# First gates of a gated recurrence one step earlier, x through GpSimd's queue, and an evenly paced weight conversion

## The chip, the cores and the metric

One core of one Trainium2 chip. The metric is the device time of one execution in microseconds (us); lower is better. Before: 490.97 us median of 3 runs (490.67 to 492.67). The engines are called as the profile calls them: PE is TensorE, DVE VectorE, ACT ScalarE, POOL GpSimd, SP SyncE.

## The reference

```python
# attention: batch 4, 8 heads, 768 positions, head size 48
for t in range(S):
    state = alpha[:, :, t, :, None] * state + einsum('bhd,bhe->bhde', k[:, :, t], v[:, :, t])
    y[:, :, t] = einsum('bhd,bhde->bhe', q[:, :, t], state)
# its output, as x (3072 tokens x 384), through a multiplicative feed-forward block
a = x @ w1          # 384 x 1024
b = x @ w2          # 384 x 1024
h = a * b @ w3      # 1024 x 1024
return h @ w_out    # 1024 x 384
# the weights are float64 in the inputs
```

## The kernel before

The sequence is cut into 24 chunks of 128 positions. **Part 1** works through them, one step n each. A step has a chain of its own: logarithm of the decay (L246, ACT), its running sum (L261, PE), exponentials (L267 and L268, ACT), their product with k and q (qk, L277, DVE), transposition (L299, PE, and its copy L301, ACT), scores (L339, PE), mask (ms, L342, DVE), attention (L364, PE), copy of the result (L368, ACT). The result, x, goes to DRAM (L236, in the next step) and comes back transposed for the **gates** (L379), in groups of three chunks. A gate half is an exact product out of three parts: six matmuls (L396), a copy (L398, ACT), three matmuls (L400), a combination (L401, DVE). Before a group's first gate its x is split in three (L385 ACT, L386 and L387 DVE).

```python
def load_x(g, queue=nc.sync):
    st["xT", g] = xp.tile([C, KM, TG], FP32, tag="xT", name="xT")
    queue.dma_start(out=st["xT", g], in_=xd[g].rearrange("(k p) t -> p k t", p=C))

def split_x(g, i):
    x = st.pop(("xT", g))
    t = tr[i].tile([C, 3, KM, TG], FP32R, tag="x3", name="x3")
    st["x3", g] = t
    nc.scalar.activation(t[:, 0], x, AF.Copy, scale=1.0 - 2.0 ** -13)            # L385
    nc.vector.tensor_sub(t[:, 1], x, t[:, 0].bitcast(FP32))                       # L386
    nc.vector.scalar_tensor_tensor(t[:, 2], t[:, 0].bitcast(FP32), 1.0 + 1.0 / P, x,
                                   op0=ALU.mult, op1=ALU.subtract)                # L387
```

Beside all that, the float64 weights are converted to fp32 by integer operations on ACT (L189, L194, L207) and DVE (3.68 us for a block), a bit in each call of `convert`. The loop that paces it:

```python
begin = {4 + 4 * g: (g, range(FH if g < 4 else KF)) for g in range(5)}

for n in range(N + 1):
    store()                       # x of the step before to DRAM, by SyncE
    ... loads of v, alpha, k and q ahead ...
    if n:
        attend_state(n - 1)
    if n < N:
        scores(n)
    transposed(n + 1)
    if n - 2 in begin:
        g, tiles = begin[n - 2]
        split_x(g, 0)
        fill.extend(gate(g, f) for f in tiles)
    pieces = (0, 3, 3, 2)[(n - 6) % 4] if n > 5 else 0
    if n == 0:
        logs(2); decays(2); logs(3)
    early = n < 7
    convert(1, 2 if n == 0 else 3)
    advance(n)
    if n:
        attend(n - 1)
    outer(n)
    run(pieces > 0)               # half a gate from the list `fill`
    if early:
        convert(1)
    decayed(n + 2)
    logs(n + 4)
    if n in begin:
        load_x(begin[n][0])
    convert(early and n > 2)
    run(pieces > 1)
    decays(n + 3)
    convert(early or n % 3 == 0)
    run(pieces > 2)
```

## Time and profile before

| | before |
|---|---|
| time, median of the first 3 runs | 490.97 us |
| span of the profiled run | 492.8 us |
| PE busy | 462.0 us, 94% |
| DVE busy | 371.0 us, 75% |
| first mask of step 11 | 94.2 us |
| first gates (L396) | 62.59 us |

The page's slices are fortieths of the span; a digit is the busy share in tenths. The rows of a stretch give its length, then busy time and number of instructions of PE, PEld, DVE, ACT and POOL, then the granted clock of TensorE (1.00 is full speed, 0.50 would be half all the time), the DMA share and GB/s. A line of a timeline gives start and length, engine, line and operation, output and inputs; in brackets how long the engine stood idle before it and what ended that. The lines themselves are shown in the prediction.

One thing to know of this profile: its run took 494.63 us, some 3 us above its neighbours. It was one execution.

### The profile page before, as it was taken

To read this page: it belongs to the slowest core of one execution; us is meant where nothing else is said; L and a number is where in the kernel's file an instruction comes from. 1 tells how busy PE (TensorE), PEld (TensorE's weight loads), DVE (VectorE), ACT (ScalarE), POOL (GpSimd) and SP (SyncE) were. 2 spreads that over 40 slices of the span, in tenths; PEclk is the share of its full clock that TensorE was granted. 3 is DMA by queue.
4 is the path that set the end of the run, shared out by engine and by line. 5 is a ranking of instruction groups with operands and counts; after the bars stand their busy time and mean duration, and the time that the engine had idled before them with its cause. 6 is when DMAs were issued, how large, how long until landed. Compare 5 with 4: busy or idle time off the path is not lost.

```text
span 492.8 us, 9909 instructions
## 1 busy us (share of the span) xinstructions
PE 462.0 (94%) x3760; PEld 422.5 (86%) x3760; DVE 371.0 (75%) x620; ACT 250.1 (51%) x479; POOL 37.5 (8%) x83
## 2 busy tenths in 40 slices
PE   3788689999998979999999999999999999999997
PEld 1566479888998968999999988888888999999996
DVE  2779899887988684999999769686433786667771
ACT  2767677676765563555556444444222533333330
POOL 2132132021103100000000000000000000000000
PEclk9989999999999998999999999999999999999999
DMA  9999999899999963666454433320001875555511
GB/s 176 185 200 205 236 199 201 217 183 234 194 227 189 214 207 101 175 183 195 158 195 155 156 117 118 118 92 32 33 32 61 229 225 176 177 176 178 176 49 48
DMA packets 160495, 79.10 MB, mean 161 GB/s; under 512 B 104640, under 2 KB 154304, under 8 KB 160448
## 3 DMA queue, kind: packets, MB, share of 16 engines
q1 hardware_dynamic: 159168, 78.40, 62.7%
q0 software_dynamic: 1280, 0.08, 0.4%
q8 instruction: 29, 0.48, 0.4%
q14 instruction: 18, 0.15, 0.1%
HBM read 56.40 MB, written 22.06 MB: 159 GB/s over the span
## 4 chain that ended last, share of the span: by engine, by line
PE 73%; DVE 9%; DMA 8%; SPq 4%; issue 3%; ACT 2%; POOL 0%; DVEq 0%; POOLq 0%; ACTq 0%
PE bank L396 37%; PE bank L400 18%; PE bank L445 8%; DMA raw<-in_moe_w_dram 3%; PE bank L339 2%; PE bank L364 2%; DVE ms L342 2%; PE bank L439 1%; DMA xT<-xd 1%; DMA abd<-ab 1%; DMA dec<-ends 1%; PE bank L299 1%; SPq L130 1%; DVE qk L277 1%; SPq L124 1%
## 5 line engine op out<-in xcount | busy, mean ns | idle before, releaser
L396 PE MATMUL bank<-x,w 128*128 128x384 f32 x768 | 159.3, 341 | 0.0
L396 PEld LDWEIGHTS bank<-x,w 128*128 128x128 f32 x768 | 134.6, 188 | 3.5 <-issue 0.5
L398 ACT ACTIVATE t<-bank 128x384 f32<-128x384 f32 x152 | 74.5, 492 | 109.7 <-PE bank L396 97.8
L401 DVE SCALAR_TENSOR_TENSOR r<-bank,t 128x384 f32<-128x384 f32 x128 | 69.7, 555 | 34.0 <-ACT t L398 32.1
L400 PE MATMUL bank<-x,w 128*128 128x384 f32 x384 | 87.3, 335 | 0.4 <-DVE x L387 0.4
L396 PE MATMUL bank<-w3o,ab 128*128 128x384 f32 x384 | 70.4, 334 | 0.0
L400 PEld LDWEIGHTS bank<-x,w 128*128 128x128 f32 x384 | 68.3, 188 | 0.7 <-issue 0.7
L396 PEld LDWEIGHTS bank<-w3o,ab 128*128 128x128 f32 x384 | 66.9, 188 | 0.0
L445 PE MATMUL bank<-wo,w3T 128*128 128x384 f32 x128 | 42.6, 486 | 0.0
L189 ACT ACTIVATE rest<-raw 128x512 f32<-128x512 uint32 (+1 forms) x36 | 23.4, 651 | 33.0 <-DMA raw<-in_moe_w_dram 20.5
L412 DVE TENSOR_TENSOR ab<-r 128x384 f32<-128x384 f32 x64 | 35.6, 556 | 2.3 <-DMA abd<-ab 1.5
L400 PE MATMUL bank<-w3o,ab 128*128 128x384 f32 x192 | 37.1, 334 | 0.0
L445 PEld LDWEIGHTS bank<-wo,w3T 128*128 128x128 f32 x128 | 24.2, 189 | 14.9
L464 DVE TENSOR_TENSOR ab<-abl,ab 128x1024 fp32r<-128x1024 f32 x24 | 29.4, 1224 | 9.2 <-ACT ab L463 9.2
L339 PEld LDWEIGHTS bank<-qkT 48*128 48x128 f32 x384 | 25.4, 200 | 12.4 <-ACT qkT L301 5.7
L339 PE MATMUL bank<-qkT 48*128 48x128 f32 x384 | 30.3, 299 | 6.0 <-ACT qkT L301 4.3
L463 ACT ACTIVATE ab<-abl 128x1024 fp32r<-128x1024 f32 x24 | 25.5, 1064 | 19.0 <-PE bank L400 18.8
L400 PEld LDWEIGHTS bank<-w3o,ab 128*128 128x128 f32 x192 | 33.6, 188 | 0.0
L342 DVE TENSOR_TENSOR ms<-bank,keep 128x512 int32<-128x512 int32 x48 | 31.1, 684 | 1.7 <-PE bank L339 1.7
L194 ACT ACTIVATE power<-power,rebias 128x512 uint32<-128x512 uint32 (+1 forms) x36 | 25.3, 705 | 12.2 <-DVE power L193 12.2
L401 DVE SCALAR_TENSOR_TENSOR o<-bank,t 128x384 f32<-128x384 f32 x24 | 13.4, 557 | 22.4 <-issue 13.7
L277 DVE TENSOR_TENSOR qk<-kq,e 128x768 f32<-128x768 f32 x24 | 22.9, 953 | 9.5 <-ACT e L268 7.2
(69 smaller groups left out, 540.1 us busy)
## 6 DMA issues: line engine op xcount, KB each, us to landing
abd<-ab SPq DMA_DIRECT2D x64, 192.0 KB, 2.7
abl<-abd SPq DMA_DIRECT2D x24, 512.0 KB, 4.5
raw<-in_moe_w_dram SPq DMA_DIRECT2D x16, 512.0 KB, 3.9
xT<-xd SPq DMA_DIRECT2D x12, 576.0 KB, 4.2
raw<-in_moe_w_dram SPq DMA_DIRECT2D x24, 256.0 KB, 4.8
ac<-in_alpha_dram SPq DMA_DIRECT2D x24, 192.0 KB, 5.0
kq<-in_k_dram SPq DMA_DIRECT2D x24, 192.0 KB, 5.4
kq<-in_q_dram SPq DMA_DIRECT2D x24, 192.0 KB, 4.3
```

The lines of the kernel that those rows point to most:

```text
L194: nc.scalar.activation(power, power, AF.Relu, scale=2.0 ** 23, bias=rebias)
L277: nc.vector.tensor_mul(qks[n % 3][:, :, :, 0:D], st.pop(("kq", n)), st.pop(("e", n)).rearrange("p i (h d) -> p i h d", h=H))
L339: nc.tensor.matmul(sc[i][:, j, :], qkT[r, 0, j, :], qkT[r, 1, j, :], start=True, stop=True)
L342: nc.vector.tensor_tensor(ms[:, i].bitcast(I32), sc[i].bitcast(I32), keep_bc, op=ALU.bitwise_and)
L396: nc.tensor.matmul(p1, w[part][i], x[part][i], start=(part == i == 0), stop=(part == 1 and i == n - 1))
L398: nc.scalar.activation(t, p1, AF.Copy, scale=(1.0 + 1.0 / P) * scale)
L400: nc.tensor.matmul(p2, w[2][i], x[2][i], start=(i == 0), stop=(i == n - 1))
L401: nc.vector.scalar_tensor_tensor(to, p2, -scale, t, op0=ALU.mult, op1=ALU.add)
L412: nc.vector.tensor_mul(ab, *r)
L445: nc.tensor.matmul(po, w3T[:, j, :], wo[:, j, :], start=(j == 0), stop=(j == KF - 1))
L463: nc.scalar.activation(t[:, 0], ab, AF.Copy, scale=1.0 - 2.0 ** -13)
L464: nc.vector.tensor_sub(t[:, 1], ab, t[:, 0].bitcast(FP32))
```

## The change

The intent: the first group's gates fill TensorE's pauses from the seventh step on, two halves in each of four steps, in place of 0+3+3+2 from there; x of part 1's groups is loaded by GpSimd's queue, so that SyncE's other loads do not stand behind it; the conversion has an even pace; logarithms and qk come earlier in their step, and the split logarithm has a second buffer. The letters A to E below are: A the second buffer, B the first group's gates, C x by GpSimd, D the order of logs and qk, E the pace of `convert`. (They are not the rivals (A) to (D) of the prediction.)

```diff
--- before.py
+++ after.py
@@ -246,7 +246,7 @@
         nc.scalar.activation(la, a, AF.Ln)
         if n >= LATE:
 
-            t = st["la", n] = work.tile([C, 2, DM], FP32R, tag="la2", name="la2", bufs=1)
+            t = st["la", n] = work.tile([C, 2, DM], FP32R, tag="la2", name="la2")
             nc.scalar.copy(t[:, 0], la)
             nc.vector.tensor_sub(t[:, 1], la, t[:, 0].bitcast(FP32))
         if n in ends:
@@ -505,7 +505,14 @@
     load_a(4)
 
 
-    begin = {4 + 4 * g: (g, range(FH if g < 4 else KF)) for g in range(5)}
+    first = 4
+    begin = {first + 4 * g: (g, range(FH if g < 4 else KF)) for g in range(5)}
+
+    def visit(n):
+        g, tiles = begin[n]
+        split_x(g, 0)
+        fill.extend(gate(g, f) for f in tiles)
+
 
     for n in range(N + 1):
         store()
@@ -517,33 +524,33 @@
         if n < N:
             scores(n)
         transposed(n + 1)
-        if n - 2 in begin:
-            g, tiles = begin[n - 2]
-            split_x(g, 0)
-            fill.extend(gate(g, f) for f in tiles)
-        pieces = (0, 3, 3, 2)[(n - 6) % 4] if n > 5 else 0
+        if n - 2 in begin and n - 2 != first:
+            visit(n - 2)
+        pieces = 0 if n <= first + 1 else 2 if n < first + 6 else (0, 3, 3, 2)[(n - first - 2) % 4]
         if n == 0:
             logs(2)
             decays(2)
-            logs(3)
-        early = n < 7
+
+        if n < 4:
+            logs(n + 3)
+        if n > 2:
+            logs(n + 4)
+        decayed(n + 2)
         convert(1, 2 if n == 0 else 3)
         advance(n)
+        if n in begin:
+            load_x(begin[n][0], nc.gpsimd)
         if n:
             attend(n - 1)
         outer(n)
         run(pieces > 0)
-        if early:
-            convert(1)
-        decayed(n + 2)
-        logs(n + 4)
-        if n in begin:
-            load_x(begin[n][0])
-        convert(early and n > 2)
+        convert(n > 0)
         run(pieces > 1)
         decays(n + 3)
-        convert(early or n % 3 == 0)
+        convert(n < 9)
         run(pieces > 2)
+        if n - 1 == first:
+            visit(first)
     store()
     part1.close()
```

## The prediction

> **What bounds the kernel now.** I read the page first (busy shares and slices), then the busy time per stretch, then the timelines of TensorE, VectorE and ScalarE over the first 200 us.
>
> The page, engine shares and slices of 12.3 us:
>
> ```profile
> PE 462.0 (94%) x3760; PEld 422.5 (86%) x3760; DVE 371.0 (75%) x620; ACT 250.1 (51%) x479; POOL 37.5 (8%) x83
> ...
> PE   3788689999998979999999999999999999999997
> ...
> DVE  2779899887988684999999769686433786667771
> ...
> PEclk9989999999999998999999999999999999999999
> ```
>
> TensorE (PE) is the bound of the whole: idle 492.8 - 462.0 = 30.8 us. The change removes no matmul, so a gain can only come out of these 30.8 us and out of matmuls that run at half clock. Where they are, from the busy time per stretch (stretch, length, busy PE, PEld, DVE, ACT, POOL, clock, DMA share, GB/s):
>
> ```profile
> 0.00:20.00 20.00, 9.07 (x70) 5.75 (x70) 7.42 (x16) 8.44 (x16) 4.03 (x21) 1.00 1.13 180
> 20.00:40.00 20.00, 17.24 (x244) 13.93 (x248) 16.26 (x29) 13.58 (x30) 5.67 (x11) 0.83 1.07 198
> 40.00:60.00 20.00, 14.48 (x246) 11.16 (x234) 18.60 (x34) 14.85 (x32) 4.17 (x8) 1.00 0.97 216
> 60.00:80.00 20.00, 18.15 (x214) 16.45 (x216) 19.77 (x36) 14.66 (x32) 5.29 (x9) 1.00 1.02 204
> 80.00:100.00 20.00, 19.98 (x269) 17.82 (x265) 18.10 (x32) 13.52 (x30) 3.88 (x5) 1.00 0.95 214
> ...
> 180.00:200.00 20.00, 17.24 (x166) 15.56 (x166) 13.32 (x25) 9.14 (x20) 0.00 (x0) 0.91 0.41 117
> 200.00:300.00 100.00, 100.00 (x565) 96.88 (x564) 91.18 (x173) 54.17 (x98) 0.00 (x0) 1.00 0.50 165
> ```
>
> 10.9 us are the start (first loads), 2.8 us lie in 20 to 40, 5.5 in 40 to 60, 1.9 in 60 to 80, about 3.3 in 80 to 180, 2.8 in 180 to 200, and the rest at the very end. Between 40 and 80 VectorE (DVE) is busy 38.4 of 40 us: there the recurrence plus the weight conversion make VectorE the bound, not TensorE. From 80 on TensorE leads with VectorE close behind; from 200 on TensorE has no gap. So only part 1 (to about 190 us) can change.
>
> The pauses themselves, from TensorE's timeline (start, length, ... idle before and what ended it):
>
> ```profile
> 49.95 0.91 PE L261 MATMUL bank<-la,after 128*128 128x384 f32 x2 [2.19 <-ACT la L246]
> 53.67 0.71 PE L299 MATMUL bank<-ident,qk 64*128 64x64 f32 x16 [1.12 <-DVE qk L277]
> 57.18 0.91 PE L261 MATMUL bank<-la,utri 128*128 128x384 f32 x2 [1.32 <-ACT la L246]
> 60.47 0.71 PE L299 MATMUL bank<-ident,qk 64*128 64x64 f32 x16 [1.28 <-DVE qk L277]
> ...
> 152.84 1.16 PE L339 MATMUL bank<-qkT 48*128 48x128 f32 x16 [1.46 <-DVE ms L342]
> ...
> 183.29 0.65 PE L358 MATMUL bank<-qkT,T 48*64 48x128 f32 x12 [1.45 <-DVE ms L342]
> 185.25 1.47 PE L339 MATMUL bank<-qkT 48*128 48x128 f32 x16 [1.30 <-ACT qkT L301]
> 186.65 1.97 PE L364 MATMUL bank<-ms,v 128*64 128x128 f32 x16
> ```
>
> Steps n = 4 to 7 pause for the step's own small chain (logs, qk), held up in VectorE's and ScalarE's order by conversion. At the end of part 1 two pauses come together, and then 16 matmuls of L364 take 1.97 us instead of 1.09: half clock. Their cause, in ScalarE's timeline:
>
> ```profile
> 183.68 0.55 ACT L189 ACTIVATE rest<-raw 128x384 f32<-128x384 uint32 x1 [1.06 <-DMA raw<-in_moe_w_out_dram]
> 184.14 1.06 ACT L301 COPY qkT<-bank 128x512 f32<-128x512 f32 x2
> ```
>
> The copy that the last scores need stands behind a conversion of w_out whose load has not landed.
>
> **What the Trainium skill says.** "TensorE: Matmul & The Clock Gate", Part 1: idleness over a window of about 3.4 us drops the array to half clock, some 3.4 us of work restore it. The trace agrees: 1.97 against 1.09 us after 2.75 us of pauses, while the lone 1.46 us at 152.84 is followed by an ordinary 1.16. The same page (Architectural detail) calls VectorE and ScalarE strictly first in, first out; the ScalarE lines above show it. "DMA: Bandwidth & Descriptors", Issuing engines are not separate DMA queues: moving a DMA to another issuer saves only issue time; and its Latency section gives the GpSimd path about 1 us to the first byte against 0.6. The list of DMA issues agrees as far as it goes: small ends<-e from GpSimd land in 3.7 us, xd<-x from SyncE in 3.9, and the xT load now in 4.2 from SyncE.
>
> **The change part by part**, worked with the instruction order of both kernels and the start-to-start times of the timeline (VectorE: mask ms 1.20 a step, qk 0.87, state 0.28, one weight block 3.68, a gate half's combination 0.47, product ab 0.47, log split 0.47, split of x 2.54; TensorE: a step about 4.2, a half gate 1.56).
>
> (1) *Gates one step earlier, 2+2+2+2 in place of 0+3+3+2.* Same 8 halves (12.5 us of TensorE). At n = 6 TensorE gets 3.1 us of work where it pauses today. But VectorE must do the split of x and 1.9 us of gate work one step earlier too. VectorE's work from the mask of step 3 to that of step 11 is 54.4 us before, and takes 94.2 - 37.2 = 57.0; after, the order gives 53.6. So at most 3.4 us are to be had, and 0.5 weight block (1.8 us) is merely put off.
>
> (2) *Even pace of conversion.* In steps 3 to 6 the order holds 12.2 us of conversion both before and after: the scheduler had already spread it, so this part does little there. It does put qk between two conversion steps, which drops two VectorE waits of 0.70 us (for ScalarE's L207). In steps 11 to 14 VectorE's work rises from 24.1 to 30.5 us, against TensorE's 4 x 4.2 + 12.5 = 29.3 and 31.4 us of time today: VectorE becomes the bound there, I say +0.6. In steps 15 to 18 it falls from 25.7 to 21.6 (29.5 us of time), so the 1.46 us at 152.84 should go: -1.3.
>
> (3) *x by GpSimd's queue.* GpSimd is idle 92%. SyncE no longer stands still at xT, and the buffer of kq comes free earlier since qk is formed earlier in the step; loads and ab stores go out sooner. But group 0's load now stands behind the save of step 8's decay (that one left at 52.1 us before) and lands, at 4.2 to 6 us, near 57 to 59. ScalarE's split (1.17) follows, so VectorE, ready near 57, waits for it: estimated 1.7 us. With that and 0.9 of small waits, stretch 3 to 11 takes 53.6 + 2.6 = 56.2: -0.8. Later groups have over ten us of slack.
>
> (4) *Second buffer of the split log, logs and qk earlier.* Waits on the one buffer in the trace are 0.8 us (ScalarE L250): hidden, about 0.
>
> (5) *End of part 1.* The weight blocks end two steps sooner (VectorE's step 15 in place of 17), so the w_out loads are issued about a step earlier, and no conversion of w_out stands right before the last L301 any more. The 1.30 us should go, the 1.45 us shrink by about 1.1 (VectorE does the whole split of x ahead of that mask, so some stays), and with them the half clock (L364 0.88, the neighbours about 1.1): 4.4 us if all happens; I take 3.5.
>
> Sum: -0.8 + 0.6 - 1.3 - 3.5 = -5.0 us; 491.0 - 5.0 = **486.0 us**.
>
> **The rivals.** (A) *The wait only changes its name*: VectorE is the bound from 40 to 125 us and has no less to do, and w_out still holds up ScalarE at the end. For it: 38.4 of 40 us busy; the end depends on where loads land. Then 489 to 491. (B) *The software queue is slow*: a 576 KB load takes several us more, VectorE stands at the split of group 0, and GpSimd, standing at that load for its source, delays the state's decay factors. For it: GpSimd is shared with those transfers, which already take 4.8 us (dec<-ends). Against: only group 0 is tight. It costs 2 to 4 us: 488 to 492. (C) *All pauses from 40 us on go*: 5.5 + 1.9 + 3.3 + 2.8 plus 2 of half clock = 15.5 us, 475.5. Against: VectorE's sums above allow at most 3.4 of the first 7.4. (D) *DMA is the bound of part 1*: its share is about 1.0 up to 160 us. Against: between 40 and 100 the pauses of TensorE end on ScalarE and VectorE; if it is so, nothing is gained: 490.
>
> **Range and chances.** Best credible case: 3.4 + 0 + 1.5 + 4.4 = 9.3 us, 481.7; worst: (B) with little at the end, 491. Range 481.5 to 491. Faster by 2% needs 481.1 or less, nearly everything at once: 0.06. Slower by 2% needs 10 us lost, which no single step here does: 0.02. Within 2%: 0.92.
>
> **What the profile after would show.** (1) First L396 of part 1 near 59 to 61 us instead of 62.6; VectorE still over 90% busy in 40 to 80. (2) Mask of step 11 at 92 to 95 us; VectorE over 90% busy in 95 to 125. (3) xT under the software queue; a wait of VectorE (or of ScalarE before it) for xT of group 0 of 1 to 3 us. (5) No L189 waiting ahead of the last L301, clock 1.00 in 180 to 200, and L364 at about 1.1 us there; part 1 over some 5 us sooner. From there on nothing changes: TensorE without a gap. I am wrong if the first gates start much later (slow queue), if steps 11 to 14 take over 33 us, or if the end of part 1 still has a half-clock stretch.

## The result, and the profile after

The changed kernel took **496.50 us** (median of 4 runs, 495.58 to 497.40), before in the same rounds 491.51 us (490.67 to 492.67): a ratio of 1.010, 95% interval 1.007 to 1.013. A ratio here is the mean time of one kernel's fast runs over that of the other's fast runs of the same rounds, so not quite the ratio of the medians. Within 2% the two count as the same, as the prediction said with 0.92; but its range ended at 491.0, and the interval says slower by about 1%.

The page after, shares and slices:

```profile
PE 469.1 (95%) x3760; PEld 427.7 (86%) x3760; DVE 372.1 (75%) x620; ACT 248.4 (50%) x479; POOL 40.2 (8%) x88
...
PE   3798699999899999999999999999999999999997
...
DVE  2679589999977676999999769686434787777771
...
PEclk9998779999899999999999999999999999999999
```

TensorE is *busier* than before by 7.1 us with the same 3760 matmuls. That is no added work: a matmul at half clock is busy longer, and the mean granted clock was 0.979 in place of 0.990. The last row says where: two slices at 0.7 from 49 to 74 us, where before had 0.9 or more.

The busy time per stretch after (columns as above):

```profile
40.00:60.00 20.00, 15.62 (x198) 12.64 (x195) 16.42 (x29) 11.19 (x25) 3.66 (x8) 0.74 1.04 225
60.00:80.00 20.00, 17.68 (x185) 15.49 (x186) 16.17 (x28) 13.08 (x28) 3.83 (x8) 0.83 0.99 208
...
180.00:200.00 20.00, 19.64 (x242) 17.95 (x239) 13.69 (x25) 9.82 (x22) 0.51 (x1) 1.00 0.34 101
```

Between 40 and 80 us VectorE, 38.4 us busy before, is busy 32.6 us: the engine that was the bound now starves. In 180 to 200 the clock is whole and TensorE's 2.8 us of pauses are 0.4.

What starves it, from TensorE's timeline after:

```profile
58.12 0.62 PE L311 MATMUL bank<-v,qk 128*64 128x48 f32 x16
62.22 2.72 PE L396 MATMUL bank<-x,w 128*128 128x384 f32 x6 [3.48 <-ACT x L385]
64.97 1.30 PE L400 MATMUL bank<-x,w 128*128 128x384 f32 x3
66.07 2.12 PE L396 MATMUL bank<-x,w 128*128 128x384 f32 x6
67.99 0.76 PE L400 MATMUL bank<-x,w 128*128 128x384 f32 x3
68.59 0.81 PE L261 MATMUL bank<-la,utri 128*128 128x384 f32 x2
69.33 1.16 PE L339 MATMUL bank<-qkT 48*128 48x128 f32 x16
```

TensorE has nothing more that it may do at 58.74, then stands 3.48 us for the split of x, and runs the first half gate at half clock (2.72 us; 1.34 before). And behind the two halves stand a decay sum, L261, which before left at 57.18 and now leaves at 68.59, and the next step's scores, L339. The mask of step 7, which needs these scores, came at 60.3 us before and at 71.6 now, and everything of VectorE that hangs on it waits with it.

The same on ScalarE:

```profile
61.01 1.16 ACT L385 ACTIVATE x<-xT 128x1152 fp32r<-128x1152 f32 x1 [2.78 <-DMA xT<-xd]
```

on VectorE:

```profile
62.20 1.36 DVE L386 TENSOR_TENSOR x<-xT,x 128x1152 fp32r<-128x1152 f32 x1 [2.19 <-ACT x L385]
```

and on GpSimd:

```profile
53.54 0.49 POOL L270 DMA_DIRECT2D ends<-e  x1 [5.47 <-ACT e L267]
54.16 0.79 POOL L379 DMA_DIRECT2D xT<-xd  x1
```

The load left GpSimd at 54.16, right behind the save of a decay (as the prediction had it), and landed 6.8 us later, at 61.0. Before, on SyncE's queue:

```profile
53.52 2.09 SPq L379 DMA_DIRECT2D xT<-xd  x1
```

on ScalarE:

```profile
59.36 1.17 ACT L385 ACTIVATE x<-xT 128x1152 fp32r<-128x1152 f32 x1 [0.35 <-DMA xT<-xd]
```

and on TensorE:

```profile
55.24 0.62 PE L311 MATMUL bank<-v,qk 128*64 128x48 f32 x16
...
62.59 1.34 PE L396 MATMUL bank<-x,w 128*128 128x384 f32 x6
```

There x left at nearly the same time, landed after 5.8 us, and TensorE asked for it only at 62.59, without a wait. (L311 is the work behind which the gates stand after the change.)

At the end of part 1, TensorE after, to be set against the pauses and the 1.97 us in the prediction:

```profile
188.70 1.16 PE L339 MATMUL bank<-qkT 48*128 48x128 f32 x16 [0.35 <-DVE ms L342]
189.79 1.09 PE L364 MATMUL bank<-ms,v 128*64 128x128 f32 x16
```

### Four stretches

A step's first mask in VectorE's timeline (L342) is a good clock of progress. The time from the start to that of step 3, from 3 to 11, 11 to 19, and 19 to the end, all from single profiled executions:

| kernel | to 3 | 3 to 11 | 11 to 19 | 19 to end | span |
|---|---|---|---|---|---|
| before | 37.2 | 57.0 | 61.0 | 337.6 | 492.8 |
| before, again | 38.0 | 57.8 | 57.7 | 337.0 | 490.6 |
| after | 37.6 | 62.6 | 61.2 | 333.1 | 494.5 |
| after, again | 37.0 | 63.1 | 61.1 | 333.5 | 494.7 |
| after, third | 39.2 | 61.8 | 61.3 | 335.0 | 497.3 |

Mean of after less mean of before: +0.3, +5.1, +1.9 and -3.5, together 3.8 us (spans: 495.5 less 491.7). The loss is in steps 3 to 11 and partly in 11 to 19; the end gains.

### The profile page after: what moved, and what is told of

The parts are those of the page before. It is cut to its first block, busy times and chain, and to the rows that moved or that the text cites. A ratio compares the mean times of both kernels' runs of the same rounds, so it can differ in the third digit from the quotient of the medians.

```text
span 494.5 us, 9907 instructions
## 1 busy us (share of the span) xinstructions
PE 469.1 (95%) x3760; PEld 427.7 (86%) x3760; DVE 372.1 (75%) x620; ACT 248.4 (50%) x479; POOL 40.2 (8%) x88
## 3 DMA queue, kind: packets, MB, share of 16 engines
q1 hardware_dynamic: 157168, 75.45, 61.1%
## 4 chain that ended last, share of the span: by engine, by line
PE 78%; DVE 6%; DMA 6%; SPq 3%; issue 3%; ACT 3%; POOL 0%; DVEq 0%; POOLq 0%; ACTq 0%
PE bank L396 39%; PE bank L400 19%; PE bank L445 8%; PE bank L364 3%; PE bank L339 3%; DMA raw<-in_moe_w_dram 2%; PE bank L299 1%; PE bank L439 1%; DMA xT<-xd 1%; DVE ms L342 1%; DMA ac<-in_alpha_dram 1%; DMA xd<-x 1%; DVE x L386 1%; PE bank L261 1%; ACT x L385 1%
## 5 line engine op out<-in xcount | busy, mean ns | idle before, releaser
L396 PE MATMUL bank<-x,w 128*128 128x384 f32 x768 | 161.3, 344 | 3.5 <-ACT x L385 3.5
L396 PEld LDWEIGHTS bank<-x,w 128*128 128x128 f32 x768 | 135.4, 190 | 7.9 <-ACT x L385 3.6
L400 PE MATMUL bank<-x,w 128*128 128x384 f32 x384 | 88.3, 338 | 1.2 <-DVE ms L342 1.2
L396 PE MATMUL bank<-w3o,ab 128*128 128x384 f32 x384 | 70.4, 334 | 0.0
L396 PEld LDWEIGHTS bank<-w3o,ab 128*128 128x128 f32 x384 | 66.9, 188 | 0.0
L464 DVE TENSOR_TENSOR ab<-abl,ab 128x1024 fp32r<-128x1024 f32 x24 | 29.4, 1224 | 8.8 <-ACT ab L463 8.6
L339 PEld LDWEIGHTS bank<-qkT 48*128 48x128 f32 x384 | 25.8, 204 | 9.9 <-issue 4.1
L339 PE MATMUL bank<-qkT 48*128 48x128 f32 x384 | 30.6, 304 | 3.1 <-ACT qkT L301 2.7
L342 DVE TENSOR_TENSOR ms<-bank,keep 128x512 int32<-128x512 int32 x48 | 30.8, 683 | 1.8 <-PE bank L339 1.6
L301 ACT COPY qkT<-bank 128x512 f32<-128x512 f32 x48 | 25.7, 588 | 11.6 <-PE bank L299 11.5
```

The costliest lines, as they stand in the source:

```text
L301: nc.scalar.copy(qkT[:, :, :, ds(DP * half, DP)], tp[half])
L339: nc.tensor.matmul(sc[i][:, j, :], qkT[r, 0, j, :], qkT[r, 1, j, :], start=True, stop=True)
L342: nc.vector.tensor_tensor(ms[:, i].bitcast(I32), sc[i].bitcast(I32), keep_bc, op=ALU.bitwise_and)
L396: nc.tensor.matmul(p1, w[part][i], x[part][i], start=(part == i == 0), stop=(part == 1 and i == n - 1))
L400: nc.tensor.matmul(p2, w[2][i], x[2][i], start=(i == 0), stop=(i == n - 1))
L464: nc.vector.tensor_sub(t[:, 1], ab, t[:, 0].bitcast(FP32))
```

## The experiments

Eighteen experiments ran: fourteen new kernels and four repeats.

### before_again and after_again, after_third: the scatter

No edit: the kernels as they are.

> The kernel before, unchanged, for its spread and a second profile. Its first profile was taken in a run of 494.6 us, 3 us over its other runs (490.7 to 492.7), with half-clock stretches at 32 to 40 and 185 to 190 us. If half clock is the difference between runs, this one shows 490 to 493 us with a mean clock above 0.990 and fewer half-clock stretches; if the profile itself costs 3 us, the clock is 0.990 again.

> The changed kernel once more, unchanged, for the scatter between chips and runs: 494.5 to 497.5 us, ratio 1.006 to 1.012; stretch 3 to 11 61 to 64 us, the clock below 0.85 between 50 and 70 us in its profile.

> The changed kernel unchanged, in the rounds of x_r4s, so that the two can be compared on one chip: ratio 1.006 to 1.010.

Measured: before_again 492.41 us, ratio to before 1.0005 (0.9957 to 1.0054). after_again 496.42, ratio 1.006 (1.0009 to 1.011); after_third 495.26, ratio 1.003 (1.0001 to 1.0059). Over everything, after has a mean of 496.2 us in 14 runs (493.8 to 499.1) and before 493.2 in 55 (490.0 to 496.3): a loss of some 3 us, less than the first 5. (after_third, at 1.003, stayed under what was expected of it; so did before_again's clock in its profile, 0.986.) Two lessons. One profile of before is not before: the pause of 1.46 us at 152.84 us, on which the prediction counted, is 0.99 us in the second and ends on another instruction (L250), and masks 15 to 19 take 28.8 us in place of 29.5. And the scatter of before goes with its clock: a line through 47 of its runs falls by 0.30 us for each 0.001 of mean granted clock (correlation -0.74), from 495.1 us on average at 0.979 to 491.9 at 0.990.

### gates_only, gates_late and gates_late2: which part loses

gates_only is before with B; gates_late, run twice (gates_late2), is after with B undone:

```diff
-        if n - 2 in begin and n - 2 != first:
+        if n - 2 in begin:
             visit(n - 2)
-        pieces = 0 if n <= first + 1 else 2 if n < first + 6 else (0, 3, 3, 2)[(n - first - 2) % 4]
+        pieces = (0, 3, 3, 2)[(n - 6) % 4] if n > 5 else 0
...
-        if n - 1 == first:
-            visit(first)
```

> The kernel before with nothing but the first group's gates one step earlier (2, 2, 2, 2 halves; x still loaded by SyncE at the old place). Theory A (the early gates stand at x, whose way through memory ends near 59 to 61 whatever queue takes it): the whole loss is here, 495 to 499. Theory B (the loss needs GpSimd's queue or the moved logs as well): 491 to 493.

> The changed kernel with group 0's gates back at 0, 3, 3, 2 halves and its split of x at the start of step 6; x still by GpSimd. Theory 1: x, landing near 60, is then needed only near 61, so nearly no wait: 489 to 493. Theory 2: as well 489 to 493, so this run alone does not part 1 and 2; with x_sync it does. Theory 3: 495 to 497.

> The changed kernel with the first group's gates at their old step, once more, in more rounds: all other parts of the change together. The first time it stood at 1.0009 of before. 0.998 to 1.003 if the gates are the whole loss; 1.004 or more if x by GpSimd or the order of logs has a share in it.

Measured: B alone costs, 495.82 us, ratio 1.0067 (1.0023 to 1.0112), stretch 3 to 11 61.9 us. All the rest without B: 493.0 us, 1.0009 (0.9966 to 1.0052), and 493.42 us, 0.9992 (0.9967 to 1.0017); 3 to 11 58.8 and 59.4 us, the end 332.8 and 332.9 us. So, by the times, **B is the loss, and everything else together is neutral**. (One trace of a kernel without B, that of late_x0_sync below, has a long stretch all the same.)

gates_late2, TensorE's timeline:

```profile
62.08 1.20 PE L364 MATMUL bank<-ms,v 128*64 128x128 f32 x12 [2.39 <-ACT e L268]
...
64.16 2.10 PE L396 MATMUL bank<-x,w 128*128 128x384 f32 x6
```

and ScalarE's:

```profile
60.49 1.16 ACT L385 ACTIVATE x<-xT 128x1152 fp32r<-128x1152 f32 x1 [2.22 <-DMA xT<-xd]
```

The late x still stops ScalarE for 2.22 us, and through the exponential behind it TensorE for 2.39, but the decay sum (L261 at 56.82) and the scores of that step have gone ahead of the gates by then. The first half gate was at half clock here too (2.10 us), without the loss.

### x_r4s, x_r3a, x_ready2, x_ready: x in time

These are the changed kernel with the first group's x loaded from an input of the same size (alpha), so that it waits for no store. Their outputs are wrong, which doesn't matter for the times. x_r4s, SyncE at the start of step 4:

```diff
         store()
+        if n == 4:
+            st["xT", 0] = xp.tile([C, KM, TG], FP32, tag="xT", name="xT")
+            nc.sync.dma_start(out=st["xT", 0], in_=alpha[0, 0:4]...)
...
-        if n in begin:
+        if n in begin and n != first:
             load_x(begin[n][0], nc.gpsimd)
```

x_r3a has it a step earlier, x_ready2 later in step 4, x_ready by GpSimd in step 2.

> The changed kernel in which group 0's x is loaded in step 2 from alpha, in the same shape (the first 384 rows of the output come out wrong on purpose), so that its gates in step 6 never wait for x. TensorE's order is the same as in the changed kernel. Theory A: no wait at the first gates, no half clock near 60, 487 to 491. Theory C (the early gates overload VectorE in steps 6 to 8 even with x there): 493 to 496. The scheduler moves the split of x up into VectorE's slack, so up to 2.5 us of what is gained can be that.

> The changed kernel, but the x of the first group is loaded from an input of the same size (alpha) by SyncE in step 4, so it hangs on no store and no load through DRAM. Wrong on purpose. Theory 1 (the early gates lose because x is not there): no wait of TensorE, VectorE or ScalarE at the first gates, clock 1.00 there, mask of step 3 to mask of step 11 in 57 to 58 us in place of 62.6, and 490.5 to 492.5 us. Theory 2 (early gates overload VectorE, the wait for x is only a symptom): 3 to 11 still takes 60 us or more, 494 to 497 us.

> The changed kernel with the x of the first group loaded by SyncE from an input of the same size at the start of step 3, some 12 us before it is needed. Wrong on purpose. If x being late is what makes the early gates lose: no wait of ScalarE for xT, the wait of TensorE at the first gates under 1 us (3.5 to 4.2 in the changed kernel), mask of step 3 to mask of step 11 in 57 to 59 us (62.6 and 63.1), mean time within 1 us of before in the same rounds (ratio 0.998 to 1.002). If early gates lose by themselves (VectorE is full there, or the gates stand ahead of the scores): 60 us and more, ratio 1.004 to 1.008.

> The changed kernel with the x of the first group loaded by SyncE from an input of the same size at the end of step 3; TensorE's order of instructions is that of the changed kernel to the last one. Wrong on purpose. Two causes are in question, and each has a size by now: x late (2 us: x_r3a 1.0043 against 1.010 and 1.006 of the changed kernel) and the early gates themselves (2 us: x_r3a against 0.9992 with late gates). If both count: x landed by 54 us, no wait for it, ratio 1.003 to 1.005, and 1.5 to 2.5 us below the changed kernel in the same rounds. If x late is all: 0.999 to 1.001. If x late is nothing: the time of the changed kernel.

| run | x landed | wait of PE at the first gates | 3 to 11 | 19 to end | median | ratio (interval) |
|---|---|---|---|---|---|---|
| after, three profiles | 61.0 to 61.7 | 3.3 to 4.2 | 61.8 to 63.1 | 333.1 to 335.0 | 496.5, 496.4, 495.3 | 1.010, 1.006, 1.003 |
| x_r4s | 54.4 | 0.47 + 0.60 + 0.57 | 59.5 | 332.7 | 494.64 | 1.001 (0.9973 to 1.0047) |
| x_r3a | 52.5 | under 0.5 | 59.9 | 335.4 | 496.17 | 1.0043 (1.0026 to 1.006) |
| x_ready2 | 57.9 | 2.21 | 59.9 | 333.3 | 494.5 | 1.003 (0.9981 to 1.0079) |
| x_ready | 9.4 | none | 57.4 | 336.7 | 495.76 | 1.0075 (1.0025 to 1.0126) |

x_r4s is the clean one: TensorE's groups of instructions are in the order of the changed kernel to the last. (ScalarE and VectorE, though, take the split of x one place earlier, ahead of a logarithm and of qk.) TensorE in it:

```profile
58.78 0.79 PE L396 MATMUL bank<-x,w 128*128 128x384 f32 x3 [0.47 <-ACT x L385]
...
62.13 1.20 PE L396 MATMUL bank<-x,w 128*128 128x384 f32 x6
...
63.69 0.81 PE L261 MATMUL bank<-la,utri 128*128 128x384 f32 x2
```

and ScalarE, which reaches L385 without a wait:

```profile
57.55 1.18 ACT L385 ACTIVATE x<-xT 128x1152 fp32r<-128x1152 f32 x1
```

The same gates stand in the same place, now at full clock, and L261 leaves at 63.69 in place of 68.59. In the traces, x in time takes the stretch from a mean of 62.5 us to 59.5. In the times of the same rounds the two (494.64 and 495.26 us) are not told apart: their intervals overlap. The traces also say what the clock has to do with it: in the stretch from 3 to 11 after, after_again and x_r3a have the same mean granted clock, 0.86, and took 62.6, 63.1 and 59.9 us; x_r4s, at 0.93, took 59.5. So about 3 us of the stretch come with the late x at one and the same clock.

The others are weaker. x_ready2 was a miss: its load stood behind SyncE's stores, left at 51.7 and landed at 57.9, so it hardly tested anything. x_ready put the load among the first ones, delayed the mask of step 3 by some 3 us (40.3), let VectorE split x in its idle start, and lost at the end. x_r3a did what was expected in 3 to 11, but moved some of TensorE's later order too and had the end of before (335.4). With x there the early gates do **not** win: none of the four is below before in its rounds.

### x_sync, store_early, old_pace: other ways to the same x

x_sync is after with `load_x(begin[n][0])` in place of `load_x(begin[n][0], nc.gpsimd)` (C undone). store_early has the first three chunks' x stored at once by GpSimd. old_pace is after with the conversion calls of before (E undone):

```diff
# store_early, in attend
+            if g == 0:
+                nc.gpsimd.dma_start(out=to[half, :, :, ds(c * C, C)], in_=x[ds(DP * half, D)])
# old_pace, in the loop
-        convert(n > 0)
+        if n < 7:
+            convert(1)
+        convert(2 < n < 7)
...
-        convert(n < 9)
+        convert(n < 7 or n % 3 == 0)
```

> The changed kernel with x of part 1 loaded by SyncE at the new place in the step. Theory 1 (x of group 0 is late by GpSimd's queue: it left at 54.2, landed at 61.0, TensorE waited 3.5 us and fell to half clock up to 68): x leaves near 52 and lands near 57, the wait falls under 1 us, time 490 to 493. Theory 2 (gates one step earlier make VectorE late whatever loads x): 495 to 497, the pause only bears another name. Theory 3 (uneven conversion in steps 11 to 14): 495 to 497.

> The changed kernel with the attention rows of group 0 (chunks 0 to 2) stored by GpSimd as soon as they are copied, in place of SyncE at the start of the next step; the result is right. The rows of chunk 2 are copied by about 41 and left only at 46 to 48, so x should land near 52 to 54 instead of 61. Theory A: first gates at about 56 to 58 without a long pause, 488 to 491, faster than before. Theory C: 493 to 496.

> The changed kernel with the calls of the conversion per step as before (2 to 4 in steps 0 to 6, then 1 or 2). Theory 1 and 2: no help, 495 to 498, as the early steps are the dense ones. Theory 3: the mask of step 15 comes 2 us sooner and the time is 492 to 494.

Measured: x_sync 496.49 us with its one slow run and 494.79 without it, 1.0054 (0.9995 to 1.0113), 3 to 11 61.7, the end 336.0. x left at 52.9 and landed at 59.1, ScalarE came to split it at 60.8, and TensorE still stood 3.8 us: **which queue loads x is not the point; the gates are too early for either.** store_early 499.47 us, 1.0134 (1.0066 to 1.0201): worse, 68.1 us in 3 to 11. The stores stand in GpSimd's order ahead of the state's decay (TensorE stood 3.83 us for it at 48.54), and ScalarE's next logarithm now stands behind L385 (TensorE's L261 stood 6.68 us for it at 61.11). old_pace 498.76 us, 1.0126 (1.0078 to 1.0175): x left at 59.0, landed at 65.3, TensorE stood 9.2 us, 3 to 11 66.2. So the even pace, whose worth alone was not run, is needed once the gates are early: in this one the steps that bring x forth were slowed by conversion.

### late_x0_sync and before_x0_sync: can the gain at the end be had alone?

late_x0_sync is gates_late with the first group's x by SyncE. before_x0_sync is before with the x of groups 1 to 4 by GpSimd:

```diff
+        if n in begin and n > 4:
+            load_x(begin[n][0], nc.gpsimd)
         if n:
             attend(n - 1)
...
-        if n in begin:
+        if n == 4:
             load_x(begin[n][0])
```

> The changed kernel with the first group's gates back at their old step (0+3+3+2 halves) and with the x of the first group loaded by SyncE, the other groups' by GpSimd. If the loss is the first group alone and the gain at the end of part 1 is x by GpSimd: stretch 3 to 11 as before (57 to 58 us), rest after the mask of step 23 304.6 us in place of 306.4, so 489.5 to 491 us, ratio 0.995 to 1.000. If the late load of the first group costs nothing when the gates are late: the same as the kernel with the late gates alone, 493.

> The kernel before, with nothing changed but that the x of groups 1 to 4 is loaded by GpSimd, at the place of the changed kernel. If the end of part 1 hangs on x by GpSimd: no conversion of w_out (L189) right ahead of the last L301, the rest after the last mask 304.6 us in place of 306.4, 489 to 490.5 us, ratio 0.995 to 0.998. If the end needs the earlier end of the weight conversion as well: 306.4 and 491.5, ratio 1.000.

Measured: 494.34 us, 1.0013 (0.9972 to 1.0053), and 494.66 us, 1.003 (0.9984 to 1.0077). Their ends are short, 333.2 and 332.4 us, so **the gain at the end comes with x by GpSimd**: gates_only and x_sync, without it, have 335.4 and 336.0. The stretch from the last mask on shows it most clearly: 306.1 to 306.4 us in the four kernels' profiles without x by GpSimd, 304.6 to 305.0 in those with it, but for x_r3a (306.1, with a pause of 1.97 us ahead of the last scores) and x_ready (305.5). TensorE in before_x0_sync, to be set against the two pauses and the 1.97 us of before:

```profile
185.58 1.16 PE L339 MATMUL bank<-qkT 48*128 48x128 f32 x16 [0.43 <-DVE ms L342]
186.68 1.09 PE L364 MATMUL bank<-ms,v 128*64 128x128 f32 x16
```

But in the times no gain is left; both runs missed what was expected of them. before_x0_sync took 60.7 us from 3 to 11 and 60.4 from 11 to 19 (before_again: 57.8 and 57.7), the first with half clock from 41.9 to 45.3 and 52.1 to 58.9 us, where nothing had been changed yet; TensorE's order is that of before to the last group. That looks like scatter of the clock, and it is as large as the gain. late_x0_sync took 62.4 us from 3 to 11, as long as after, with the gates at their old step: x had landed at 59.6, but a conversion stood ahead of its split in ScalarE's order, and TensorE stood at the first gates once more:

```profile
64.92 1.10 PE L396 MATMUL bank<-x,w 128*128 128x384 f32 x3 [1.88 <-ACT x L385]
```

So a single profile of this stretch does not single out B; the times of the kernels with and without it do.

### warm, warm2 and before_warm: is it the half clock?

Matmuls for nothing (128x128) ahead of TensorE's pauses: 24 ahead of the first gates (warm), 10 ahead of each of four decay sums and 12 ahead of the first gates (warm2), and 10 ahead of four decay sums in before_x0_sync (before_warm, whose edit is shown):

```diff
         la = st.pop(("la", n))
+        if 5 < n < 10:
+            idle = bank()
+            for _ in range(10):
+                nc.tensor.matmul(idle[:, 0:C], utri, utri, start=True, stop=True)
```

> The changed kernel with 24 matmuls of 128x128, whose result nobody reads, ahead of the first gates in step 6, so that TensorE is busy while it waits for x. If half clock after the pause (51 to 68 us) is most of the loss: 492 to 494. If the wait itself is: 495.5 to 498.

> The changed kernel with idle-time matmuls for nothing (10 of 128x128 ahead of the decay sums issued in steps 2 to 5, 12 ahead of the first gates), so that TensorE has fewer pauses. If the loss is mainly half clock: mean granted clock 0.986 or more in place of 0.978, and 493 to 494.5 us, although some 1 to 2 us of work are added. If it is the waits themselves: clock up, time unchanged at 495.5 to 497.5.

> The kernel before with the x of groups 1 to 4 loaded by GpSimd, and with 10 matmuls for nothing ahead of the decay sums issued in steps 3 to 6, where its own half clock lies. The times of before run from 490.0 to 496.3 us and fall by 0.31 us for each 0.001 of granted clock. If that is cause and not company: clock 0.990 or more, 490 to 491.5 us, ratio 0.994 to 0.998. If the added matmuls cost what they give: ratio 1.000 to 1.004.

Measured: warm 494.71 us, 1.005 (1.0001 to 1.01), mean clock 0.988 in place of 0.979, 3 to 11 61.2 us. warm2 504.95 us, 1.0222 (1.0205 to 1.024), clock 0.988. before_warm 498.57 us, 1.0096 (1.0066 to 1.0126), clock 0.990. The clock rose and the time did not fall; warm came out between its two theories. I had mis-sized the filler: in before_warm, TensorE's timeline,

```profile
37.80 2.50 PE L263 MATMUL bank<-utri 128*128 128x128 f32 x20
44.54 2.50 PE L263 MATMUL bank<-utri 128*128 128x128 f32 x20
```

and the stretch from 40 to 60,

```profile
40.00:60.00 20.00, 19.07 (x284) 16.25 (x283) 17.94 (x31) 13.00 (x28) 3.69 (x6) 1.00 1.01 235
```

ten of them take 2.50 us (an fp32 matmul stands as two instructions in the trace, hence x20), so 10.0 us were added (13 us in warm2). By their ratios, taken in other rounds, before_warm lost 0.0066 of the time, some 3 us, against before_x0_sync; the intervals just overlap. So **part of what is put ahead of the decay sums seems to land on the path, though TensorE was pausing there**, even with a better clock. That is B's lesson with other work.

## Why the prediction was wrong

**Steps (1) and (3), the first gates and x by GpSimd: the step that failed.** It gave stretch 3 to 11 as 53.6 + 2.6 = 56.2 us and -0.8; measured 62.5 and +5.1. It named the right events: x under the software queue, behind the save of step 8's decay, ScalarE standing for it (said 1 to 3 us, measured 2.78). It failed first in the time of landing: "4.2 to 6 us, near 57 to 59" began at the median of twelve loads, where in before's trace this load took 5.8, and x landed at 61.0. It failed above all in what it let the wait cost, for it priced it as VectorE's alone, 1.7 us. TensorE takes its matmuls strictly in order (the Trainium skill, "TensorE: Matmul & The Clock Gate", Part 3, The mechanism; this trace agrees, L261 left only behind the gates), so 3.48 us of standing plus two half gates at half clock fell on the recurrence. The sum of VectorE's work, from which 56.2 came, was not the trouble (it was busy 55.0 us in the stretch, 54.9 before), but it is no estimate of the time when VectorE starves: its busy share from 40 to 80, which should have stayed over 90%, was 81%. The evidence was there to see: in before's trace TensorE was done with L311, behind which the gates were to stand, at 55.86, and x landed only at 59.34, with ScalarE's split still to come.

With x in time the stretch is 59.5 to 59.9 in the two runs that test it; with the gates late 58.8 and 59.4 (62.4 in late_x0_sync); before 57.0 and 57.8. So x being late is some 2.8 us of the 5.1 (62.5 less the mean of 59.5 and 59.9), by the traces. How the other 2 us divide between the early gates themselves, x by GpSimd, the order of logs and scatter stays open. So does the clock's own share in the whole: after runs at a mean clock of 0.979, before at 0.985, which by before's slope would go with 0.006 x 300 = 1.8 us; but that slope is company, not proof, and the three fillers could not separate the two.

**Step (2), the pace.** It said +0.6 in 11 to 14 and -1.3 after; measured together +1.9 for 11 to 19. VectorE was busy 98% in 95 to 125, as predicted, and in all three traces of after TensorE stood 1.29 us for a mask (L342) at about 128 us. The pause at 152.84, the -1.3, did go, but masks 15 to 19 took 29.4 to 29.7 us all the same (before 29.5 and 28.8). Kernels with x by GpSimd mostly have 59 to 61 us here, those without 57.6 (x_sync) and 58.7 (gates_only), but before itself has 61.0 and 57.7, so what costs it is not settled.

**Step (4).** Not run alone. With everything but B neutral, no cost or gain of it is seen.

**Step (5), the end of part 1: right** in kind and in size, but not in its cause: -3.5 said, -3.5 measured for step 19 to the end, no half clock there, the pauses 0.35 us in place of 2.75, L364 back at 1.09 us. (The three ends of after lie 2 us apart, so that it fits to the tenth is luck.) It put the gain down to the weight blocks' earlier end. In x_sync the last block was in step 15, as said, and the last L364 still took 1.40 us; in before_x0_sync it stayed in step 17, and the pauses and the half clock were gone. So the gain goes with x by GpSimd, which the prediction had not counted there. But part 1 ended later, not sooner (mask of step 23 at 189.9 against 186.7), because of (1) to (3).

**The rivals.** (B) was nearest, with its slow queue and its early x; but the queue is not what mattered (x_sync), and its 2 to 4 us were too few. (A) is half right: VectorE had nothing to gain. (C) and (D) did not happen.

No kernel beats before by more than the scatter; the best, gates_late2, is at 0.9992 (0.9967 to 1.0017).

## What to carry to other kernels

Before work is moved forward into an engine's pause, follow its input back to its source and compare the time it lands with the time the engine would reach the work; and ask what stands behind it in the order of that engine, for that is what pays. A pause inside a step's own chain is not free room. Profile the kernel before more than once before you count on a single pause: here one of the predicted gains hung on a pause that was a third shorter in the second profile, and it did not come.

## What the Trainium skill lacked or had wrong

- "TensorE: Matmul & The Clock Gate", Part 1: right that pauses bring half clock (L396 2.72 us in place of 1.34), and its window of about 3.4 us fits: each half-clock stretch inside these spans lasted 3.41 us or two, three or six times that. But its table asks for an idle window, and less was enough here: one pause of 1.64 us at the end of part 1 in gates_only, and one of 1.82 in x_sync, were followed by half clock (L364 1.88 and 1.40 us in place of 1.09). So the 2.75 us in the prediction do not agree with it as fully as was said there. What it lacks is what that does to a comparison: with pauses of 1 to 2.5 us strewn over some steps, the same kernel has a mean clock of 0.979 in one run and 0.993 in another, and 490.0 to 496.3 us.
- The same page has no price for filler in fp32: keeping the clock up with matmuls for nothing cost 2.50 us for ten of 128x128, and the time rose (ratio 1.0096 against 1.003 without them, in other rounds) while the clock went from 0.981 to 0.990.
- "DMA: Bandwidth & Descriptors", Latency and other measured facts: a first byte at 1 us from GpSimd against 0.6 from SyncE. For the 576 KB of the first x, with the DMA share at about 1.0, the spread between runs was larger than that: 5.9, 6.8 and 7.6 us from GpSimd, 4.9 and 5.8 from SyncE before, 6.2 from SyncE in x_sync. The section has 0.2 us for an access to HBM and 2 us at high load; what busy DMA engines add to a transfer of this size no page says.
- "DMA: Bandwidth & Descriptors", Issuing engines are not separate DMA queues: in keeping with the first group (the early gates lost with SyncE's queue too, 1.0067 in gates_only), but it lacks that a change of issuer reorders everything else in that issuer's line. In before_x0_sync, where nothing else was changed, the fifth load of w_out left at 174.1 us in place of 179.7, no conversion stood ahead of the last copy, and the rest from the last mask on took 304.6 us in place of 306.1.
